# FNet and GEGLU layers on one core: issue order at the seams between token halves

## The chip, the cores and the metric

The kernel runs on one core of a Trainium2 chip. The core has TensorE (PE, matmuls into eight PSUM banks), VectorE (DVE), ScalarE (ACT), GpSimd (POOL) and SyncE (SP); the last two issue most of the transfers, which share 16 DMA engines. The metric is the device time of one execution in microseconds. The time before is the median of three runs, 1607.92 us (1604.04 to 1608.05).

## The reference

Four layers on x of 2048 tokens by 512, in fp32; the first and third mix with a discrete Fourier transform, the second and fourth are a gated feed-forward.

```python
def _A_ref(x, dft_seq_re, dft_seq_im, dft_hid_re, dft_hid_im):
    a = jnp.einsum("bsd,ed->bse", x, dft_hid_re)
    b = jnp.einsum("bsd,ed->bse", x, dft_hid_im)
    y = jnp.einsum("ts,bse->bte", dft_seq_re, a) - jnp.einsum("ts,bse->bte", dft_seq_im, b)
    return y

def _B_ref(x, w_gate, w_up, w_down):
    return (_gelu(x @ w_gate) * (x @ w_up)) @ w_down      # F = 1792

x = A_x
x = x + _A_ref(_layernorm(x), ...)
x = x + _B_ref(_layernorm(x), B_w_gate, B_w_up, B_w_down)
x = x + _A_ref(_layernorm(x), ...)
x = x + _B_ref(_layernorm(x), B_w_gate, B_w_up, B_w_down)
```

## The kernel before

**Precision.** Every fp32 operand is split in two parts of a shorter type: ScalarE copies the high part (line 151), VectorE subtracts it from the source (line 153). A product `mm3` (lines 208 to 210) is then three matmuls of 128x128 by 128x512: high by high, high by low, low by high. A split therefore costs one instruction on each of two engines, and a product of two 128-row pieces costs six matmuls.

**Layers.** Layers 0 and 2 (the numbers in the code) are the mixing layers, `mix`, 1728 matmuls each. Layers 1 and 3 are the feed-forward, `geglu(w, layer)`, called for two halves of 1024 tokens, w = 0 and 1. Matrix products are done by a Strassen scheme (Winograd's form) with seven products in place of eight: A11, A12, S1 to S4, A22 on the side of the weights, B11, B21, B22, T1 to T4 on the side of the activations.

**One half of a feed-forward layer.** The gate and up projections are 14 chunks, `up(n)`, of seven products of six matmuls (`product`, named after the weight block). The loop is skewed: `first(n + 1)` (A11 by B11, then its bank copied into another one by `seed`, line 202) and `second(n + 1)` (A12 by B21) of the next chunk are written in the middle of `up(n)`. Results leave PSUM by ScalarE copies (`copied`, line 195), gelu (line 1019) and VectorE (lines 188 and 1033). Beside the chunks, `beside(n)` runs w_down's products A11 and A12, one for each chunk; the rest of w_down, 36 products in a list `late` in layer 1 and in the first half of layer 3, comes after chunk 13. Each late product takes one piece of w_down, loaded by SP (line 327, `s<-wc`), and one split activation block, made by `prepared`. When the seven products of a kind are done, `ended` adds banks together and transposes them into the rows of x (lines 188, 1264, 191).

**The norm of a half.** For the next half, eight blocks of 128 rows of x are normed (`norm(i)` in `block_steps`): four transfers of 32 rows each load the block three norms ahead (line 245), ScalarE makes the statistics (line 564 is the first of them, lines 565, 566 and 569 follow, with two tiny POOL operations between), ScalarE applies them (line 590), VectorE transposes (line 672) and POOL writes every fourth block to memory (line 675). `fetch(c)` then reads the blocks back turned (line 686, SP), and `first(c)`, `second(c)`, `fourth(c)` and `divide` make the differences and splits for B11 to T4. These are the z blocks.

**Who runs when.** Work beside the products stands in two lists. Each `product` and each late product calls `step()`, which runs one entry of `queue`, and at every `pace[0]`-th call one entry of `slow`. In a first half, `slow` gets the eight norms with a pace of 9; in a second half before a mixing layer it gets four empty entries and the eight `terms_ahead` (the statistics for the mixing layer's first rows) with a pace of 7. After the chunks, `queue` gets the fetches and z blocks, four empty entries ahead of them. In layer 3 the fetches come already with chunk 13. At a third of the late products, eight loads of the next half's weights (`ahead`, line 1009, `s<-wb`) are laid between the entries. A rule at the end of the loop runs two entries per product where the list would otherwise outlast it.

**Order.** All this is the order in which the program is written. The build reorders it: each engine's instructions are put in the order in which a timing model finds them ready, with the written order as priority. An instruction that the model holds for ready early can so stand on its engine ahead of much that is written before it; on the chip an engine then waits at it. `tc.issue_after(ins)` ties what is written inside the block, on the engine of `ins`, to come behind `ins` on that engine; it waits for nothing else. `paced(run)` does this with the newest split on ScalarE and on VectorE. It is used before for the rows that return to the mixing layer.

Of the kernel before, what the change touches and what calls it, by code (L numbers as in the profile page):

```python
# [17 lines left out]
ND = D // P  # L18
# [19 lines left out]
FORE = {0: 4, 2: 4}  # L38
MADE = 5
LEAD = 3  # L40
NK = NS // 2
SEED_AT = 3
MIXED = 4
# [4 lines left out]
def fnet_geglu(ctx: ExitStack, tc: tile.TileContext, x_in, ws, wh, wgu, wdn, wdc, out):  # L48
# [32 lines left out]
    nc = tc.nc  # L81
# [65 lines left out]
    newest = {}  # L147
# [7 lines left out]
    def paced(run):  # L155

        def paced_run():
            with tc.issue_after(newest["ACT"].ins), tc.issue_after(newest["DVE"].ins):
                run()
        return paced_run  # L160
# [37 lines left out]
    def seed(ps, src):  # L198

        inside = id(src) in ps8.held  # L200
        with ExitStack() if inside else behind("ACT"):
            i = nc.scalar.activation(ps, src, AF.Copy)  # L202
        if inside:
            bank_read["ACT"] = i

    def mm3(ps, a, b, start, stop):
        (ah, al), (bh, bl) = a, b
        nc.tensor.matmul(ps, ah, bh, start=start, stop=False, skip_group_check=True)  # L208
        nc.tensor.matmul(ps, ah, bl, start=False, stop=False, skip_group_check=True)  # L209
        nc.tensor.matmul(ps, al, bh, start=False, stop=stop, skip_group_check=True)  # L210

    half = slice(0, 256), slice(256, 512)

# [20 lines left out]
    def x_load(layer, i, engine=nc.sync):  # L234
        t = sb.get()
        engine.dma_start(t, rows(layer, i))
        return t
# [137 lines left out]
    def make_a11(k):  # L375

        def run(v):
            held[k] = v
            return split_slot(v)
        return run  # L380
# [42 lines left out]
    def skewed(n):  # L423

        skew = SKEW[n - 2]
        return [(i, k - i * skew) for k in range(NK + (n - 1) * skew) for i in range(n) if 0 <= k - i * skew < NK]

# [14 lines left out]
    def bare(layer, b, what, k):  # L442

        return layer == 0 and b == 0 and what == "A11" and k < 6
# [4 lines left out]
    def down_order(layer, w):  # L449
        n = SEVEN[layer, w]  # L450
        up = [(name, k) for k in range(n) for name in ("A11", "A12")]
        if n < NP:
            late = [("S2", k) for k in range(n)] + [("S1", 0)] + [("S3", k) for k in range(n)] + [("S1", 1)]
            late += [("A22", k) for k in range(n - 1)] + [("S1", k) for k in range(2, n)]
            return up, late + [("A22", n - 1)] + [("S4", k) for k in range(n)]
        late = [("S1", k) for k in range(LEAD)]
        late += [p for k in range(n) for p in [("S2", k)] + [("S1", k + LEAD)] * (k + LEAD < n)]
        late.insert(LEAD + 2, up.pop())
        late += [("S4", k) for k in range(2)]
# [4 lines left out]
    def mix_items(layer):  # L464
        def raw(make, *tiles):
            items.append((F32, tiles, make, None))

        for b, what in plan(layer):
            tiles = [[ws[(b * 2 + m) * NS + k] for k in range(NS)] for m in range(2)]
            (a11, a12), (a21, a22) = ((r[:NK], r[NK:]) for r in tiles)  # L470
            hold = b >= FORE[layer]
            if what == "A11":
                for k in range(NK):
                    raw(as_is if bare(layer, b, what, k) else make_a11(k) if hold else plain, a11[k])
            elif what == "A12":
                for k in range(NK):
                    raw(plain, a12[k])
# [35 lines left out]
    queue, slow, steps_done, pace, down_making = [], [], [0], [PACE], []  # L513
# [19 lines left out]
    def norm_terms(layer, i, x, junk):  # L533
# [3 lines left out]
        shift = pool.tile([P, 1], F32, name="shift")  # L537
        if layer == 0 or layer == 2 and i >= NS - NK:
            st = spool.tile([P, 6], F32, name="st")
# [32 lines left out]
    def terms_ahead(layer, i, n):  # L572

        if i == 0:
            fresh["terms"] = x_load(layer, 0)
        x, junk = fresh.pop("terms"), sb.get()
        if i + 1 < n:
            fresh["terms"] = x_load(layer, i + 1)
        known[layer, i] = norm_terms(layer, i, x, junk)
        sb.put(x, junk)  # L580
# [23 lines left out]
    def first_rows(layer, k):  # L604
        for i in range(k if k == 0 else k + 2, min(k + 3, NK)):
            fresh[i] = x_load(layer, i)
        first_norm(layer, k)
        first_parts(k)
# [8 lines left out]
    def second_rows(layer, k):  # L617
        if NK + k not in fresh:
            fresh[NK + k] = x_load(layer, NK + k, nc.gpsimd)
        second_norm(layer, k)  # L620
        second_parts(k)
# [13 lines left out]
    def combine_late(k):  # L635
        u = t34.pop(k)
        zparts["T34", k] = split_slot(u)
        sb.put(u)
# [377 lines left out]
    def activated(g):  # L1016
# [2 lines left out]
        nc.scalar.activation(t, g, AF.Gelu_apprx_tanh)  # L1019
        return t  # L1020

    def geglu(w, layer):

        gs, h, acc = {}, {}, {0: [], 1: []}

        def finished(n, second, part, v):

            f = n // 2 * 2 + second
            if n % 2 == 0:
                gs[f, part] = activated(v)  # L1030
            else:
                t = h[f, part] = gs.pop((f, part))
                nc.vector.tensor_tensor(t, t, v, op=ALU.mult)  # L1033
# [32 lines left out]
        def product(n, ps, an, bn, start, stop):  # L1066
            step()
            hi, lo = wparts[n][an]
            for c in range(2):
                cut = slice(c * P, (c + 1) * P)  # L1070
                mm3(ps, (hi[:, cut], lo[:, cut]), blocks[bn, c], start and c == 0, stop and c == 1)
            if an in ends:
                i = ends[an]
                sb.put(*wparts[n][i])
                if not making and n + 2 < NF:
                    piece_load(n + 2, i)

        def first(n):
            if n < NF:
                chain[n] = ps8.get()  # L1080
                product(n, chain[n], "A11", "B11", True, True)
                c11[n] = ps8.get()
                seed(c11[n], chain[n])

        def second(n):
            if n < NF:
                ps = c11.pop(n)
                product(n, ps, "A12", "B21", False, True)
                finished(n, 0, 0, ps)
                ps8.put(ps)  # L1090
# [49 lines left out]
        def down(f, part):  # L1140
            for _ in down_steps(f, part):
                pass
            step()
# [134 lines left out]
        def add_rows(part, keep=False):  # L1278
            for i in range(NT):
                x_add(layer, (w * 2 + part) * NT + i, xrows.pop(0), acc[part][i], keep)  # L1280
# [39 lines left out]
        before_mix = w == 1 and layer < 3  # L1320
        plain_down = (layer, w) not in SEVEN
        if before_mix:
            slow.extend([lambda: None] * 4 + [(lambda k=k: terms_ahead(layer + 1, k, NK)) for k in range(NK)])
            pace[0] = 7
        if w == 0:
            pace[0] = PACE
            norms, others = block_steps(layer, 1)
            slow.extend(norms)
            ahead_of_all = others[:ND] if layer in (3,) else []
        if not plain_down and layer == 1 or layer == 3:  # L1330
            sb.reclaim("x")
        first(0)
        second(0)
        for n in range(NF):
            if w == 0 and n == NF - 1 and ahead_of_all:
                while slow:
# [10 lines left out]
        elif pairs == NP:  # L1347
            load_turned(0)
        if w == 0:
            queue.extend([None] * 4 + others[len(ahead_of_all):ND] + ([] if ahead_of_all else [None] * 4) + others[ND:])  # L1350
        elif before_mix:
            queue.extend((lambda k=k: first_rows(layer + 1, k)) for k in range(NK))
        ahead = [(lambda n=n, i=i: piece_load(n, i)) for n in range(2) for i in range(len(pieces))]
        if plain_down:
            for f in range(NF - LAG, NF):
                down(f, 0)
            add_rows(0)
            if before_mix:
                for k in range(NT):
                    queue.extend([lambda k=k: second_rows(layer + 1, k), lambda k=k: combine(k)])  # L1360
                queue.extend([lambda k=k: combine_late(k) for k in range(NT)])
            else:
                queue.extend(ahead)
            for f in range(NF):
                if f == NF - 2:
                    load_rows(1)
                down(f, 1)
                while len(queue) > 2 * (NF - 1 - f):
                    step()
            add_rows(1, before_mix)  # L1370
        else:
            if pairs == NP:
                pair_combined(NP - 1)
            late = down_order(layer, w)[1]
            for i, (name, k) in enumerate(late):
                for more in late[i:i + EARLY + 1]:
                    prepared(*more)
                for _ in down_product(name, k):
                    pass
                if not before_mix or i % 3 == 0:  # L1380
                    step()
                if before_mix and i == len(late) // 2:
                    stream["more"] = MORE
                if i == len(late) // 3:
                    load_turned(1)
                    if w == 0:
                        queue[:2 * len(ahead)] = [run for pair in zip(ahead, queue) for run in pair] + queue[len(ahead):2 * len(ahead)]
                while w == 0 and len(queue) > 2 * (len(late) - 1 - i):
                    step()
            if pairs < NP:  # L1390
                plain_rows()
# [24 lines left out]
    ps = ps8.get()  # L1416
# [91 lines left out]
```

## Time and profile before

| | us |
|---|---|
| median of three runs | 1607.92 |
| lowest, highest | 1604.04, 1608.05 |
| profiled execution, its own time | 1607.73 |
| its span, from first to last instruction | 1606.0 |
| TensorE busy | 1596.6 |
| VectorE, ScalarE, GpSimd busy | 1133.2, 884.5, 275.3 |
| longest transfers: pieces of w_down, 182 of 256 KB, issue to landing | 4.7 |
| mean granted clock of TensorE | 0.998 |

How to read it: a row of a timeline gives start, length, engine, line, operation, output and inputs, how many alike follow one another, and in brackets the idle time of the engine ahead of it and what ended it. `PE` rows are matmuls; their lengths overlap, so the distance of two starts is the pace. `SPq` rows are the issues of transfers by SyncE. `issue` as the reason of a wait is time for which the profile shows no releasing instruction. A row of stretches gives the busy time of each engine and the number of its instructions that touch the stretch, so that one matmul at each edge is counted in two stretches.

### The profile page before, as it was taken

Reading aid. Unit: us, or ns where it says so; the run is one execution under the profiler, and the core shown is the slowest. Engines: PE = TensorE matmul, PEld = TensorE weight load, DVE = VectorE, ACT = ScalarE, POOL = GpSimd, SP = SyncE. Lnnn points to the kernel's source line nnn. Section 1 sums busy time; section 2 is a strip of 40 time slices with the busy share of each in tenths; the row PEclk is TensorE's granted clock in tenths of the full one; section 3 lists DMA queues with packets and bytes.
Section 4 is the critical chain, followed back from the end, with each engine's and each line's share of the span. In section 5 each row is a group of like instructions: output and inputs, shape, how many; then the busy total and the mean of one; then the engine's idle time right before and its main releaser. Section 6 shows DMA issues by size and latency. Waiting matters only on the chain. (4 is left out here: it accounts for less than half of the span.)

```text
span 1606.0 us, 22616 instructions
## 1 busy us (share of the span) xinstructions
PE 1596.6 (99%) x7008; PEld 1316.2 (82%) x7008; DVE 1133.2 (71%) x1958; ACT 884.5 (55%) x1711; POOL 275.3 (17%) x469
## 2 busy tenths in 40 slices
PE   9999999999999999999999999999999999999998
PEld 7888888888888888888888888888887888888887
DVE  7997878887699783455879877777744447744574
ACT  8955565654767554546666636565545545433460
POOL 4112121352456101000040001101410000000001
PEclk9999999999999999999999999999999999999999
DMA  9878888996998899855896776878989576895445
GB/s 360 295 259 306 296 300 286 353 308 199 334 349 322 267 360 298 232 164 177 280 310 196 250 254 217 301 240 294 260 285 281 185 212 192 312 300 173 125 151 157
DMA packets 238872, 419.14 MB, mean 261 GB/s; under 512 B 28512, under 2 KB 66656, under 8 KB 237728
## 3 DMA queue, kind: packets, MB, share of 16 engines
q1 hardware_dynamic: 214512, 336.16, 65.0%
q0 software_dynamic: 24240, 81.55, 14.4%
q8 instruction: 55, 0.90, 0.2%
q14 instruction: 65, 0.53, 0.1%
HBM read 341.31 MB, written 76.28 MB: 260 GB/s over the span
## 5 line engine op out<-in xcount | busy, mean ns | idle before, releaser
L209 PE MATMUL p<-s,s 128*128 128x512 f32 x2320 | 900.2, 389 | 0.0
L210 PE MATMUL p<-s,s 128*128 128x512 f32 x2320 | 893.5, 389 | 0.0
L208 PE MATMUL p<-s,s 128*128 128x512 f32 x2320 | 868.0, 390 | 3.7 <-ACT s L195 2.3
L153 DVE TENSOR_TENSOR s<-s,s 128x512 fp32r<-128x512 f32 (+1 forms) x809 | 508.8, 663 | 127.4 <-ACT s L151 113.2
L151 ACT ACTIVATE s<-s 128x512 fp32r<-128x512 f32 (+1 forms) x809 | 455.4, 607 | 243.9 <-DVE s L184 66.4
L208 PEld LDWEIGHTS p<-s,s 128*128 128x128 f32 x2320 | 435.8, 188 | 96.9 <-ACT s L195 3.4
L209 PEld LDWEIGHTS p<-s,s 128*128 128x128 f32 x2320 | 435.8, 188 | 90.9 <-DVE s L153 0.4
L210 PEld LDWEIGHTS p<-s,s 128*128 128x128 f32 x2320 | 435.8, 188 | 90.5
L188 DVE TENSOR_TENSOR s<-s,p 128x512 f32<-128x512 f32 x188 | 127.2, 684 | 166.8 <-PE p L210 137.6
L184 DVE TENSOR_TENSOR s<-s,s 128x512 f32<-128x512 f32 (+1 forms) x374 | 223.3, 614 | 5.8 <-DMA s<-t 3.7
L195 ACT ACTIVATE s<-p 128x512 f32<-128x512 f32 x232 | 134.2, 594 | 129.7 <-PE p L210 125.9
L567 POOL TENSOR_SCALAR rstd<-rstd 128x1 f32<-128x1 f32 x40 | 24.9, 623 | 367.1 <-ACT s L566 352.2
L1019 ACT ACTIVATE s<-s 128x512 f32<-128x512 f32 x84 | 52.8, 629 | 57.9 <-DVE s L188 48.2
L153 DVE TENSOR_TENSOR s<-xwide,s 128x512 fp32r<-128x512 f32 x71 | 47.8, 681 | 35.6 <-ACT s L151 35.4
L1033 DVE TENSOR_TENSOR s<-s,p 128x512 f32<-128x512 f32 x56 | 38.4, 685 | 33.6 <-PE p L210 31.7
L313 POOL DMA_DIRECT2D wb<-s x84 | 46.2, 552 | 89.8 <-ACT s L151 67.5
L1019 ACT ACTIVATE s<-p 128x512 f32<-128x512 f32 x28 | 16.7, 597 | 67.1 <-PE p L210 65.2
L151 ACT ACTIVATE s<-xwide 128x512 fp32r<-128x512 f32 x71 | 43.2, 621 | 17.9 <-DVE xwide L184 9.4
L590 ACT ACTIVATE s<-s,shift,rstd 128x512 f32<-128x512 f32 x56 | 44.9, 811 | 10.2 <-DMA s<-x 4.8
L202 ACT ACTIVATE p<-p 128x512 f32<-128x512 f32 x56 | 32.8, 586 | 30.3 <-PE p L210 30.0
L191 DVE TENSOR_TENSOR s<-s,s 128x512 f32<-128x512 f32 (+1 forms) x68 | 40.7, 607 | 6.8 <-DMA s<-ws 4.5
L564 ACT ACTIVATE s<-s 128x512 f32<-128x512 f32 x33 | 20.7, 627 | 36.9 <-PE p L209 15.6
(100 smaller groups left out, 612.6 us busy)
## 6 DMA issues: line engine op xcount, KB each, us to landing
s<-ws SPq DMA_DIRECT2D x384, 256.0 KB, 4.9
s<-wb SPq DMA_DIRECT2D x294, 256.0 KB, 5.2
s<-wc SPq DMA_DIRECT2D x182, 256.0 KB, 4.7
s<-wh SPq DMA_DIRECT2D x116, 256.0 KB, 4.9
wb<-s POOLq DMA_DIRECT2D x98, 256.0 KB, 5.4
s<-x SPq DMA_DIRECT2D x59, 256.0 KB, 5.2
xwide<-ws SPq DMA_DIRECT2D x50, 256.0 KB, 4.9
wc<-s POOLq DMA_DIRECT2D x49, 256.0 KB, 5.1
```

The lines of the kernel that those rows point to most:

```text
L151: newest["ACT"] = nc.scalar.activation(hi, src, AF.Copy)
L153: newest["DVE"] = nc.vector.tensor_tensor(lo, src, f32(hi), op=ALU.subtract)
L184: nc.vector.tensor_tensor(out, a, b, op=ALU.subtract)
L188: bank_read["DVE"] = nc.vector.tensor_tensor(out, a, b, op=ALU.add)
L191: nc.vector.tensor_tensor(out, a, b, op=ALU.add)
L195: bank_read["ACT"] = nc.scalar.activation(v, src, AF.Copy)
L208: nc.tensor.matmul(ps, ah, bh, start=start, stop=False, skip_group_check=True)
L209: nc.tensor.matmul(ps, ah, bl, start=False, stop=False, skip_group_check=True)
L210: nc.tensor.matmul(ps, al, bh, start=False, stop=stop, skip_group_check=True)
L313: nc.gpsimd.dma_start(a, f32(t))
L590: nc.scalar.activation(z, x, AF.Identity, bias=shift, scale=rstd)
L1019: nc.scalar.activation(t, g, AF.Gelu_apprx_tanh)
```

## The change

Four places, all about order; no arithmetic changes.

```diff
+HOLD = 12
...
-        nc.tensor.matmul(ps, al, bh, start=False, stop=stop, skip_group_check=True)
+        newest["PE"] = nc.tensor.matmul(ps, al, bh, start=False, stop=stop, skip_group_check=True)
...
+    late_end = []
...
         if before_mix:
-            slow.extend([lambda: None] * 4 + [(lambda k=k: terms_ahead(layer + 1, k, NK)) for k in range(NK)])
+            slow.extend([lambda: None] * 4 + [paced(lambda k=k: terms_ahead(layer + 1, k, NK)) for k in range(NK)])
             pace[0] = 7
         if w == 0:
             pace[0] = PACE
             norms, others = block_steps(layer, 1)
-            slow.extend(norms)
+            slow.extend(paced(run) if layer == 3 else run for run in norms)
...
-        first(0)
-        second(0)
+        with tc.issue_after(late_end.pop().ins) if late_end else ExitStack():
+            first(0)
+            second(0)
...
         if w == 0:
-            queue.extend([None] * 4 + others[len(ahead_of_all):ND] + ([] if ahead_of_all else [None] * 4) + others[ND:])
+            queue.extend([None] * 9 + others[len(ahead_of_all):ND] + ([] if ahead_of_all else [None] * 4) + others[ND:])
...
                 for _ in down_product(name, k):
                     pass
+                if i == len(late) - HOLD:
+                    late_end.append(newest["PE"])
```

- The norms of layer 3's first half (which prepare its second) and the statistics ahead of the mixing layer, in layer 1's second half, are `paced`: on ScalarE and VectorE they come behind the newest split that is written before them.
- The z blocks (in layer 1 with their fetches) are written five steps later in the late products.
- `first(0)` and `second(0)` of a half come, on TensorE, behind the last matmul of the late product that is twelfth from the end in the list of the half before (number 24 of 0 to 35). A matmul is noted in every half; what layer 1's second half notes is used by layer 3's first half, a whole mixing layer later, and that of the last half by none.

## The prediction

> **What bounds the kernel now.** I read the page's head first, then the busy time of each engine in stretches that I cut where TensorE stops being full, and then the order of time around each cut.
>
> ```profile
> span 1606.0 us, 22616 instructions
> PE 1596.6 (99%) x7008; PEld 1316.2 (82%) x7008; DVE 1133.2 (71%) x1958; ACT 884.5 (55%) x1711; POOL 275.3 (17%) x469
> ```
>
> ```profile
> 0.00:40.00 40.00, 38.65 (x149) 28.22 (x150) 31.90 (x79) 33.41 (x63) 19.31 (x42) 1.00 0.99 359
> 40.00:400.00 360.00, 360.00 (x1590) 298.10 (x1589) 303.50 (x531) 216.18 (x421) 87.94 (x135) 1.00 0.84 290
> 400.00:440.00 40.00, 39.91 (x177) 32.72 (x176) 27.74 (x52) 30.70 (x65) 18.79 (x36) 1.00 1.01 325
> 440.00:760.00 320.00, 320.00 (x1414) 264.96 (x1413) 214.70 (x367) 182.80 (x367) 70.58 (x118) 1.00 0.83 271
> 760.00:800.00 40.00, 39.23 (x173) 32.20 (x172) 35.35 (x61) 26.61 (x49) 0.00 (x0) 1.00 0.84 294
> 800.00:1200.00 400.00, 400.00 (x1766) 331.07 (x1765) 302.20 (x535) 222.83 (x437) 60.01 (x106) 1.00 0.79 259
> 1200.00:1240.00 40.00, 37.69 (x160) 30.64 (x158) 14.96 (x23) 20.27 (x44) 3.72 (x7) 0.96 1.07 283
> 1240.00:1360.00 120.00, 120.00 (x531) 99.38 (x530) 66.01 (x102) 58.63 (x109) 2.84 (x7) 1.00 0.64 196
> 1360.00:1400.00 40.00, 39.47 (x175) 32.27 (x174) 33.98 (x56) 21.94 (x40) 0.00 (x0) 1.00 0.90 315
> 1400.00:1600.00 200.00, 200.00 (x884) 165.62 (x883) 100.16 (x154) 71.10 (x125) 12.12 (x20) 1.00 0.61 184
> 1600.00:1606.00 6.00, 1.64 (x8) 1.02 (x6) 2.66 (x4) 0.00 (x0) 0.00 (x0) 0.80 0.64 249
> ```
>
> The columns are length, then busy time and count of PE, weight loads, DVE, ACT and POOL, then granted clock, DMA share and GB/s. The number of matmuls is fixed, and in full stretches they start 400/1764 = 0.2268 us apart (1766 less the two at the edges). So the time is 7008 matmuls plus whatever TensorE waits, and between the opening and the tail it waits in four stretches only: those at 400, 760, 1200 and 1360. The one at 1200 is by far the largest (160 matmuls where 178 fit), and the only one with a clock below full. Nothing that keeps TensorE fed elsewhere can gain anything; any new wait costs its whole length.
>
> The stretch at 1200, on ScalarE and then on TensorE:
>
> ```profile
> 1217.17 0.57 ACT L1019 ACTIVATE s<-p 128x512 f32<-128x512 f32 x1
> 1222.25 0.63 ACT L564 ACTIVATE s<-s 128x512 f32<-128x512 f32 x1 [4.51 <-issue]
> 1222.88 0.58 ACT L195 ACTIVATE s<-p 128x512 f32<-128x512 f32 x1
> ```
>
> ```profile
> 1220.82 0.39 PE L210 MATMUL p<-s,s 128*128 128x512 f32 x1
> 1223.51 0.50 PE L208 MATMUL p<-s,s 128*128 128x512 f32 x1 [2.31 <-ACT s L195]
> ...
> 1224.81 0.63 PE L210 MATMUL p<-s,s 128*128 128x512 f32 x1
> ...
> 1227.80 0.79 PE L208 MATMUL p<-s,s 128*128 128x512 f32 x2
> 1228.43 0.40 PE L209 MATMUL p<-s,s 128*128 128x512 f32 x1
> ```
>
> ```profile
> 1216.51 7.15 SPq L245 DMA_DIRECT2D s<-x  x8
> ```
>
> ScalarE stands idle for 4.51 us ahead of line 564, the first statistic of a norm, while the copy of a finished PSUM bank (line 195) stands behind it. TensorE needs that bank. The norm reads rows of x by line 245, whose eight issues take until 1223.66. So a norm that is wanted much later came to the head of ScalarE's queue before its rows had landed.
>
> **The change, part by part.** It adds and removes no instruction of any engine; it adds order alone.
>
> *Norms of layer 3's second half.* Where are they wanted? The last matmul starts 0.39 before 1601.64, at 1601.25. Layer 3 has 882 + 894 = 1776 matmuls (14 chunks of 42, then 49 w_down products of 6; in the second half 35 of 6 and 96 of plain rows). At 0.2268 that is 402.8, and with some 5 us of waits (below) layer 3 starts at 1601.3 - 402.8 - 5.0 = 1193.5. A norm runs at every 9th step; a chunk has 7 steps and 48 matmuls (42 in the first).
>
> ```profile
> L564 ACT ACTIVATE s<-s x8: 617/632/634, 1184.6 to 1281.0; 128x512 f32<-128x512 f32 x8
> ```
>
> The eight are spread from 1184.6 to 1281.0; the one at 1222.25 is the fifth, by the timeline's order. The fifth norm's step is the 37th to 45th, that is after 42 + 4x48 = 234 to about 300 matmuls: 1247 to 1266. It ran 25 to 44 us early. With the change it stands on ScalarE behind the newest split, that of A11 of pair 2, whose data are finished in chunk 4 (42 + 3x48 + 30 = 216 matmuls, 1242 at the earliest). Its rows were all issued by 1223.66, so it would no longer find them missing, and the bank copies of chunks 2 to 4 no longer stand behind it.
>
> What goes with that wait, from the rows: 1223.51 - 1220.82 - 0.227 = 2.46; then five starts in 1.30 where 1.13 is usual, 0.17; then nine starts from 1224.81 to 1228.43, 3.62 where 2.04 is usual, 1.58. Together **4.21 us**. The last piece is the clock:
>
> ```profile
> 1224.80:1228.20 3.40, 3.40 (x10) 2.60 (x9) 1.96 (x4) 2.08 (x5) 0.52 (x1) 0.51 1.02 222
> ```
>
> By the Trainium skill (TensorE: Matmul & The Clock Gate, "Part 1: The HAM clock gate"), the clock halves after an idle window of about 3.4 us, free-running, and matmuls of 512 columns then start 426.7 ns apart; the trace agrees on the pitch (1224.81 to 1225.24 and on, 0.43), but here a wait of under 2.7 us was enough. By the page's window the stall would be worth 2.46 + 0.17 = 2.6 and the sum below would end at 1604.3; I go by the rows.
>
> Cost of the move itself: eight norms of about five ScalarE operations, four DMAs each for their rows (not held back, since they are SP's) and a transpose on DVE go to 1202 to 1310, where ACT is busy 58.6 of 120 and DVE 66.0. Behind a held norm on ScalarE stand only bank copies and gelus, and the norm waits for a split that comes before them in the program anyway. Bounds: 0, or again one wait of 4.21 if some other late input now stands at the head. I take 0. The last norm then ends some 23 us later than 1281, near 1305, and its block is fetched from chunk 13, at about 1193.5 + 4 + 618x0.2268 = 1338: 33 us of room.
>
> *Statistics ahead of the mixing layer* (layer 1, second half, 600 to 730): TensorE is full from 440 to 760, so this can gain nothing there; ACT is busy 182.8 of 320, so it costs nothing either. Taken at 0; bounds 0 and one wait of 1.04 (the price of the wait at 766, below).
>
> *Blocks of the next half five steps later.* A step comes with each late product, 6 x 0.2268 = 1.36, so 6.8 us. In layer 1 the last split before the second half (1601.3 - 402.8 - 5.0, less 1728 + 882 matmuls and a wait of 1.04: 600.5) is
>
> ```profile
> 594.88 0.69 DVE L153 TENSOR_TENSOR s<-s,s 128x512 fp32r<-128x512 f32 x1
> ```
>
> Even if that is the last block it ends at 595.6 + 6.8 = 602.4, and in the order of the program S1 needs its block 18 matmuls into the half, at 604.6. The cover is the row of A22 products at the end of the late stage (7 x 1.36 = 9.5 us). 0, and if the cover were gone, 6.8 per half at most.
>
> *First products behind the twelfth late product from the end.* This is where the order on TensorE changes. The late stage of layer 3 before:
>
> ```profile
> 1348.00:1360.00 12.00, 12.00 (x55) 9.93 (x54) 11.55 (x20) 6.29 (x12) 0.00 (x0) 1.00 0.90 286
> 1360.00:1372.00 12.00, 11.47 (x51) 9.10 (x50) 12.00 (x21) 8.81 (x18) 0.00 (x0) 1.00 1.05 386
> 1372.00:1380.00 8.00, 8.00 (x37) 6.62 (x36) 7.61 (x14) 6.33 (x13) 0.00 (x0) 1.00 0.91 317
> 1380.00:1392.00 12.00, 12.00 (x54) 9.95 (x53) 7.28 (x12) 5.40 (x9) 0.00 (x0) 1.00 0.68 216
> ```
>
> ```profile
> L202 ACT ACTIVATE p<-p x2: 579/588/597, 1364.0 to 1396.6; 128x512 f32<-128x512 f32 x2
> ```
>
> ```profile
> L202 ACT ACTIVATE p<-p x2: 582/582/582, 586.8 to 598.1; 128x512 f32<-128x512 f32 x2
> ```
>
> Line 202 copies a first product into the bank of the next: its rows date the next half's first product at 1364.0 and, in layer 1, at 586.8. The halves begin by count at 1193.5 + 882x0.2268 + 5 = 1398.5 and 600.5, and twelve products before are 1382.2 and 584.2. So the hold bites in layer 3, by 18 us or more, and hardly in layer 1. There DVE is full from 1348 to 1380 and DMA above 0.9; the wait in this stretch is for a piece of w_down:
>
> ```profile
> 1362.65 0.61 PE L208 MATMUL p<-s,s 128*128 128x512 f32 x2
> 1363.79 0.50 PE L208 MATMUL p<-s,s 128*128 128x512 f32 x1 [0.53 <-DMA s<-wc]
> ```
>
> ```profile
> 1356.29 3.30 SPq L327 DMA_DIRECT2D s<-wc  x5
> 1359.71 1.03 SPq L1009 DMA_DIRECT2D s<-wb  x2
> ```
>
> Lost: 1363.79 - 1362.88 - 0.23 = 0.68, and 0.11 at the next start, 0.8. Its loads (line 327) are issued between those of the next half, each when its buffer is released by DVE or ACT. With block work five steps down in priority, DVE's eleven or so block operations of 1348 to 1360 make room for the late splits, the buffers come free sooner, and TensorE needs no filler. Bounds: a gain of 0.8; a loss of the filler, between the 6 matmuls that must lie ahead of 1364.0 (1.4 us) and the 30 that the program puts ahead of the second seed at 1396.6 (6.8 us). I take the gain, since DVE has 4.7 of 12 us free from 1380 to 1392, where the moved work goes.
>
> The third wait stays as it is:
>
> ```profile
> 764.29 1.07 PE L208 MATMUL p<-s,s 128*128 128x512 f32 x4
> 766.12 0.50 PE L208 MATMUL p<-s,s 128*128 128x512 f32 x1 [0.77 <-DMA s<-wc]
> ```
>
> (766.12 - 764.97 - 0.23 + 0.11 = 1.04; no hold applies there.)
>
> **The sum.** Own time of the profiled execution 1607.73 (span 1606.0 and 1.73 around it) - 4.21 - 0.80 = 1602.7. The median of the runs, 1607.92, is 0.2 above the profiled one, so I say **1602.8**, 0.32% below the median. A measurement of this kernel tells about 0.3% from no change, 4.8 us, so the forecast stands just beyond that line.
>
> **The rivals.** *Only the norm's wait goes*: the wait for w_down stays or moves, and small new ones come, as any new order brings: 1603.5 and up to 1607, no change that can be told. For it: DMA is at 1.05 from 1360, whatever the order on TensorE. Against it: the load in question was late in issue, not only in transfer.
>
> *The cover is lost* (the other side): with the next half's products held, TensorE runs into late products whose splits or pieces are not there. Place: 1361 to 1375, and the like in layer 1; price 6.8 + 1.4, and after each the slow clock, 1.75 as above: 1607.7 - 4.2 + 8.2 + 3.5 = 1615.2. It decides as soon as the late splits on DVE fall more than the two or three products that are ready in advance (about 4 us) behind. For it: DVE at 12.00 of 12. Against it: the block work that fills DVE is pushed back by 6.8 us at the same time. By the page above, waits this short would leave the clock alone, and this case would be 1611.7.
>
> *The pin does not hold*: the newest split could itself run early, the fifth norm with it, and the wait stays: 1607. Against it: that split needs chunk 4's product.
>
> **How the numbers follow.** Forecast 0.48 (1601.7, with the wait at 766 gone too, to 1603.1), only the norm's wait 0.22, pin without effect 0.06, cover lost 0.24. Faster by over 0.3% 0.47, within 0.28, slower 0.25. The range: the lowest is 1601.7, and a run more or less favourable (the runs shown reach from 1604.0 to 1608.1) takes it to 1600.5; above it takes in the second and third case and the smaller losses of the cover, to 1613. The likeliest case alone: 1601 to 1604.
>
> **What would show it.** Right: the stretch 1200 to 1240 with 178 matmuls at clock 1.00, line 564's fifth row after 1240, no 4.51 ahead of it; line 202's first row of the second half after 1380, and no wait for wc near 1363. Wrong: line 195 or 564 again ahead of a matmul; a wait for line 153 or for wc between 1360 and 1400; a clock below 1.00 in any slice after the opening.

## The result, and the profile after

| | before | after |
|---|---|---|
| median, us (nine runs each, the first three of before included) | 1607.92 | 1602.85 |
| lowest to highest | 1604.04 to 1609.71 | 1601.86 to 1604.44 |
| profiled span | 1606.0 | 1601.0 |

The ratio of the times is 0.9971, with a 95% interval of 0.9961 to 0.9981. The forecast was 1602.8. The busy time by stretch of the changed kernel, cut at the same places (length, then PE, weight loads, DVE, ACT, POOL, granted clock, DMA share, GB/s):

```profile
span 1601.0 us, 22648 instructions
```

```profile
400.00:440.00 40.00, 39.91 (x176) 32.73 (x176) 27.74 (x52) 30.70 (x65) 18.73 (x36) 1.00 1.01 320
440.00:760.00 320.00, 320.00 (x1414) 265.05 (x1413) 214.64 (x368) 183.04 (x366) 69.60 (x117) 1.00 0.84 271
760.00:800.00 40.00, 39.29 (x174) 32.20 (x173) 34.69 (x60) 26.47 (x49) 0.00 (x0) 1.00 0.86 295
800.00:1200.00 400.00, 400.00 (x1766) 331.09 (x1765) 301.52 (x535) 221.22 (x430) 57.99 (x104) 1.00 0.78 259
1200.00:1240.00 40.00, 40.00 (x178) 33.12 (x177) 18.96 (x28) 21.22 (x46) 2.85 (x7) 1.00 0.95 246
1240.00:1360.00 120.00, 120.00 (x531) 99.41 (x530) 68.10 (x106) 63.79 (x123) 3.57 (x9) 1.00 0.72 228
1360.00:1400.00 40.00, 40.00 (x178) 33.15 (x177) 31.38 (x51) 15.87 (x28) 2.64 (x4) 1.00 0.90 307
```

Two of the four stretches in which TensorE waited are full now: that at 1200 (178 matmuls for 160, clock 1.00) and that at 1360. Those at 400 and 760 are as they were. Below are the fifth statistic of layer 3's norms, on ScalarE (line 565 now, since the code lies one to six lines lower), and the copies of the first products of the next halves, in layer 3 and in layer 1 (line 203 was 202):

```profile
1240.93 0.63 ACT L152 ACTIVATE s<-s 128x512 fp32r<-128x512 f32 x1 [1.48 <-DVE s L1036]
1241.46 0.61 ACT L565 ACTIVATE s<-s 128x512 f32<-128x512 f32 x1
```

```profile
L203 ACT ACTIVATE p<-p x2: 582/582/582, 1387.0 to 1387.8; 128x512 f32<-128x512 f32 x2
L203 ACT ACTIVATE p<-p x2: 582/582/582, 593.1 to 594.7; 128x512 f32<-128x512 f32 x2
```

The statistic stands right behind a split and waits for nothing, 19 us later than before. The first copy of layer 3's second half moved from 1364.0 to 1387.0, that of layer 1's from 586.8 to 593.1. In layer 1 it was the later blocks that moved it, not the hold: without the hold it is at 593.4 (run 3), without the later blocks at 586.7 (run 4). Which part bought the time is another matter.

### The profile page after: what moved, and what is told of

Its sections match the earlier page's. It is cut to its first block, busy times and chain, and to the rows that moved or that the text cites. A ratio compares the mean times of both kernels' runs of the same rounds, so it can differ in the third digit from the quotient of the medians.

```text
span 1601.0 us, 22648 instructions
## 1 busy us (share of the span) xinstructions
PE 1594.2 (100%) x7008; PEld 1315.2 (82%) x7008; DVE 1132.7 (71%) x1958; ACT 883.7 (55%) x1711; POOL 271.5 (17%) x469
## 4 chain that ended last, share of the span: by engine, by line
PE 93%; DMA 3%; issue 2%; POOL 1%; ACT 0%; DVE 0%; SPq 0%; POOLq 0%; ACTq 0%; DVEq 0%
PE p L210 31%; PE p L211 31%; PE p L209 31%; DMA s<-t 1%; PE p L810 1%; DMA s<-x 1%; DMA s<-ws 0%; DMA s<-wc 0%; POOL rstd L568 0%; DMA xwide<-ws 0%; ACT s L152 0%; POOL s L687 0%; POOL wb L314 0%; DVE s L154 0%; ACT xwide L196 0%
## 5 line engine op out<-in xcount | busy, mean ns | idle before, releaser
L1020 ACT ACTIVATE s<-s 128x512 f32<-128x512 f32 x84 | 52.8, 629 | 47.1 <-DVE s L189 44.6
L980 POOL DMA_DIRECT2D wc<-s x42 | 30.5, 728 | 53.8 <-ACT s L152 36.4
```

## The experiments

Ratios are to runs of the kernel before on the same chip; where no interval is given there is one run and its profile. "By starts" means the distance of two starts less the usual 0.23 us. In the fourteen profiles the 201st matmul starts between 51.6 and 52.3 us, though no edit touches what comes before it: a difference under 0.7 us between the spans of two single executions tells nothing. "The stretch at 1200" is the wait behind line 564, "at 1360" the wait for a piece of w_down.

**1. The pin on layer 3's norms alone.**

```diff
-            slow.extend(norms)
+            slow.extend(paced(run) if layer == 3 else run for run in norms)
```

> The kernel before with the pin on layer 3's norms alone. My theory (the pin takes 4.2 us, the later blocks with the held products 0.8): about 1603.5 us, TensorE full from 1200 to 1240 at clock 1.00, and a wait of 0.5 to 1 us for a piece of w_down (wc) still there near 1360. Rival A (the pin alone does everything, by its shift of the schedule): 1602.8 and no wait near 1360. Rival B (the norm's wait goes because of the later blocks or the held products): no better than 1607.

1603.11 us, ratio 0.9977 (0.9967 to 0.9987).

```profile
1200.00:1240.00 40.00, 40.00 (x178) 33.15 (x177) 18.20 (x27) 19.24 (x39) 1.50 (x4) 1.00 1.03 267
1360.00:1400.00 40.00, 40.00 (x178) 33.15 (x177) 28.71 (x47) 17.25 (x30) 2.64 (x4) 1.00 0.88 305
```

Both stretches are full. Rival A holds: with the pin alone neither wait is there, so the later blocks and the hold are not needed for the one at 1360 to go. (Run 8 shows that this wait can also be missing without the pin.)

**2. All but that pin.**

```diff
-            slow.extend(paced(run) if layer == 3 else run for run in norms)
+            slow.extend(norms)
```

> The kernel after without the pin on layer 3's norms. My theory: the wait of about 2.5 us for the bank copy behind line 564 is back near 1223 with the slow clock behind it, the wait near 1360 stays gone: about 1607 us. Rival B (other parts of the change removed it): no such wait, 1603 us.

1602.78 us, ratio 0.9970 (0.9960 to 0.9979): my theory missed this one. The wait is gone without the pin. The list of ScalarE shows how:

```profile
1221.93 0.58 ACT L203 ACTIVATE p<-p 128x512 f32<-128x512 f32 x1 [0.16 <-PE p L211]
...
1227.19 0.63 ACT L152 ACTIVATE s<-s 128x512 fp32r<-128x512 f32 x1 [1.19 <-DVE s L1036]
1227.88 0.63 ACT L565 ACTIVATE s<-s 128x512 f32<-128x512 f32 x1
```

The fifth statistic is still early, but it starts at 1227.88 and not at 1222.25, and it finds its rows there (no wait in brackets). The rest of the change moved it by 5.6 us without meaning to. Its rows came sooner too: the last of its four transfers was issued at 1214.07 and landed at 1218.22; before it was issued at 1214.30 and landed at 1222.18.

**3. All but the hold.**

```diff
-        with tc.issue_after(late_end.pop().ins) if late_end else ExitStack():
+        with ExitStack():
```

> The kernel after without the hold on the next half's first products. My theory: the later blocks already let the late splits through, so no wait of TensorE near 1360 even with the first product early (line 202's first row near 1360): the span within 0.3 us of the changed kernel's 1601.0. Rival C (the hold is what removes the wait, since the early first product and its weights crowd out w_down's pieces): a wait for wc of 0.5 to 1 us comes back between 1350 and 1370, span about 1601.8.

1603.26 us in one run, span 1601.5, 0.5 over the change's where I had allowed 0.3. The first product is early again (line 203's first row at 1362.9), and TensorE has no wait at 1360. So nothing here speaks for rival C, that the early first product delays the piece of w_down. The wait at 766 is 0.5 us longer (1.2 us for wc, 0.7 with the change), a place that no part of the change names; it also differs by 0.3 us between profiles whose order up to there is the same (0.77 before, 0.45 in run 1).

**4. All but the later blocks.**

```diff
-            queue.extend([None] * 9 + others[len(ahead_of_all):ND] + ([] if ahead_of_all else [None] * 4) + others[ND:])
+            queue.extend([None] * 4 + others[len(ahead_of_all):ND] + ([] if ahead_of_all else [None] * 4) + others[ND:])
```

> The kernel after with the blocks at their old place (four empty steps). My theory: DVE is again full of block work ahead of the late splits, and with the first products held TensorE has less to fill with: a wait between 1350 and 1380 of 0.8 to 5 us, span 1601.8 to 1606. Rival C (the hold alone does it): no wait, span 1601.0.

1603.97 us in one run, span 1602.2:

```profile
1356.95 0.61 PE L209 MATMUL p<-s,s 128*128 128x512 f32 x2
1358.22 0.50 PE L209 MATMUL p<-s,s 128*128 128x512 f32 x1 [0.66 <-DMA s<-wc]
```

A wait for wc is back at this seam, 0.8 us by starts (1358.22 - 1357.18 - 0.23). Run 9, which has both pins but no hold, has none. This fits a hold that makes the wait and later blocks that pay for it, but it rests on one profile each.

**5. The pin on the fifth norm only.**

```diff
-            slow.extend(norms)
+            slow.extend(paced(run) if layer == 3 and k == 4 else run for k, run in enumerate(norms))
```

> The kernel before with the pin on the fifth of layer 3's eight norms alone. Theory D (the wait is a meeting of one early statistic with one late block of rows; whatever puts that one statistic later removes it): no wait near 1223, clock 1.00 from 1200 to 1240, about 1603.5 us, a wait for wc near 1360 left or not. Rival (the pin works by the shift of all eight norms, or another norm takes the fifth's place at the head): a wait of 2 us or more between 1200 and 1280 is left, 1606 us or more.

1603.70 us, ratio 0.9968 (0.9957 to 0.9980). No wait at 1200 and none at 1360; one statistic of eight is enough, so the price was that of a single meeting. Here the last of its rows landed at 1224.97, no sooner than before, but the statistic stood at 1252.17: it is its place that counts. But the profiled execution (1605.15) has a wait that before's did not show, in layer 1:

```profile
635.41 0.63 ACT L564 ACTIVATE s<-s 128x512 f32<-128x512 f32 x1 [6.11 <-DMA s<-x]
```

```profile
PE p L208 <- ACT s L151: 1.7, 1, 1.7
```

This is the first of the statistics ahead of the mixing layer, at the head of ScalarE 6 us ahead of its row; ScalarE worked almost without a pause after it, and the split that TensorE needed came late. Up to 1170 every engine has the order of the kernel before, by line, operation and tile, so up to here these are two executions of one order: the row was issued at 629.08 here and at 625.58 before, and landed about 6 us later in both.

**6 and 7. The later blocks alone, the hold alone.** Each is its line of the diff in the kernel before.

> The kernel before with the later blocks alone. Theory D: moving the blocks in layer 1 shifts the order of all that follows, so that the fifth statistic, though not pinned, starts after its rows have landed, as it did without the pin (statistic at 1227.9, rows at 1218.2): no wait near 1223, about 1603 us. Rival (the hold on the first products or the pinned statistics did that): the wait near 1223 is there, 1607 us.

1605.68 us, ratio 0.9990 (0.9979 to 1.0000).

```profile
1200.00:1240.00 40.00, 40.00 (x178) 33.08 (x177) 15.18 (x22) 24.53 (x52) 5.18 (x11) 1.00 1.01 303
600.00:640.00 40.00, 36.48 (x154) 29.71 (x153) 13.99 (x21) 13.85 (x30) 6.17 (x12) 0.96 1.06 291
```

As theory D said, the stretch at 1200 is full without any pin; the time is not the 1603 that it gave. The gain is lost again at 634.90, where a bank copy stood behind the first statistic of layer 1 (6.46 us on its row) and TensorE waited 3.5 us, with the slow clock after it.

> The kernel before with the hold on the first products alone. Theory D: the order of layer 3's norms is that of the kernel before, so the wait near 1223 stays, with the slow clock: 1605 to 1608 us. With the blocks at their old place and the first products held, the wait for wc near 1360 stays too (0.8) or grows. Rival (the hold shifts the schedule enough): no wait near 1223, 1603 us.

1608.97 us in one run. The waits of TensorE in it (who waited for whom, in all, times, longest):

```profile
PE p L209 <- ACT s L196: 2.1, 1, 2.1
PE p L209 <- DMA s<-wc: 2.0, 2, 1.2
```

The wait at 1200 stays, that at 1360 is 1.4 by starts where it was 0.8, and one of 0.8 by starts stands at 633. The time lies a little above what I expected, but within the runs of the kernel before on that chip (1604.94 to 1612.05): that the hold alone loses is not shown.

**8. The pin on layer 1's statistics alone.**

```diff
-            slow.extend([lambda: None] * 4 + [(lambda k=k: terms_ahead(layer + 1, k, NK)) for k in range(NK)])
+            slow.extend([lambda: None] * 4 + [paced(lambda k=k: terms_ahead(layer + 1, k, NK)) for k in range(NK)])
```

> The kernel before with the pinned statistics ahead of the mixing layer alone. I hold that they neither gain nor cost: TensorE full from 600 to 760 as before, the wait near 766 between 0.7 and 1.5 us, and the wait near 1223 still there with the slow clock: 1605 to 1608 us. Rival: they are what moves the wait near 1223, 1603 us.

1605.41 us in one run. The wait near 1223 is there, shorter (1.5 us), and the slow clock that I expected with it did not come but for a matmul or two:

```profile
1221.54 0.39 PE L210 MATMUL p<-s,s 128*128 128x512 f32 x1
1223.42 0.50 PE L208 MATMUL p<-s,s 128*128 128x512 f32 x1 [1.49 <-ACT s L195]
```

From 740 to the end this kernel has the order of the kernel before on every engine, by line, operation and tile. So the same order cost a wait of 1.65 us by starts here, and 2.46 with the slow clock behind it, 4.21 in all, in the profile before. And the wait at 1360 is not there: the only wait of TensorE for a piece of w_down in the whole execution is that at 766 (in all, times, longest).

```profile
PE p L208 <- DMA s<-wc: 0.7, 1, 0.7
```

**9. Both pins, without hold and later blocks.**

> The kernel before with both pins (layer 3's norms, and the statistics ahead of the mixing layer), without the hold and with the blocks at their old place. Theory E (the pins do all of it: a statistic at the head of ScalarE ahead of its rows is the only thing that costs more than 1 us, once near 1223 and, in some executions, near 633): 1602.5 to 1603.3 us, all runs within 3 us of each other, no wait near 1360 as with the norms' pin alone. Rival F (the hold and the later blocks carry part of the gain): 1604 us or more.

1603.33 us, ratio 0.9975 (0.9964 to 0.9986), the runs within 2 us (1602.74 to 1604.66), no wait at 633, 1223 or 1360. The interval overlaps that of the whole change, so no contribution of the hold and the later blocks together can be told.

**10. All but the pin on layer 1's statistics.**

> The kernel after without the pin on the statistics ahead of the mixing layer. Theory E: the first of them waits on ScalarE for its row again (issued near 625, landed 5.7 to 8.2 us later in the runs so far), and in some executions TensorE waits 1 to 5 us near 633: median 1603 to 1605, runs 3 us or more apart. My prediction's view (this pin is worth nothing): 1602.8, spread as with the change.

1604.63 us, ratio 0.9980 (0.9972 to 0.9989); runs from 1603.53 to 1605.97, so the median is as theory E said and the spread, 2.4, less. On ScalarE and TensorE:

```profile
631.35 0.63 ACT L565 ACTIVATE s<-s 128x512 f32<-128x512 f32 x1 [4.04 <-DMA s<-x]
631.89 0.19 ACT L565 ACTIVATION_READ_ACCUMULATOR s<-s 128x1 f32 x1
631.98 0.58 ACT L196 ACTIVATE s<-p 128x512 f32<-128x512 f32 x1
```

```profile
631.13 0.39 PE L211 MATMUL p<-s,s 128*128 128x512 f32 x1
632.61 0.50 PE L209 MATMUL p<-s,s 128*128 128x512 f32 x1 [1.09 <-ACT s L196]
```

It is the picture of 1223 once more, statistic, bank copy, matmul: 1.25 us by starts. This pin takes away a wait that my prediction put at nothing. What it is worth in the median is not settled: the interval overlaps those of the whole change and of run 9, and in this profile 0.8 us more than with the change went to the wait at 766, which the pin does not touch.

**11. The norms of layer 1's first half pinned too** (an attempt at the wait near 405).

```diff
-            slow.extend(paced(run) if layer == 3 else run for run in norms)
+            slow.extend(paced(run) for run in norms)
```

> The kernel after with the norms of layer 1's first half pinned as well. If the wait near 405 (0.36 us after a bank copy that stands behind a norm's statistic written later) has the same cause, it goes, and the time is 0.4 to 0.5 us less: 1602.4 us. Rival (the wait there comes from the copies of the mixing layer's rows, or the moved norms make another): as the change, 1602.8, or up to 2 us more.

1604.72 us, ratio 0.9979 (0.9970 to 0.9988): 1.9 us above the change by medians, with intervals that overlap. The stretch 400 to 440 is full, so the cause was guessed rightly, but two new waits came:

```profile
585.89 0.50 PE L209 MATMUL p<-s,s 128*128 128x512 f32 x1 [0.95 <-DMA s<-wc]
...
588.60 0.50 PE L209 MATMUL p<-s,s 128*128 128x512 f32 x1 [1.05 <-DMA s<-wc]
```

They are for pieces of w_down in layer 1's late stage, 2.3 us by starts. What was saved is less than half a microsecond: before, two starts near 405 stand 0.48 and 0.34 us apart where 0.23 is usual, 0.36 in all.

**12. The hold behind the very last late product** (`HOLD = 1`).

> The kernel after with the next half's first products held behind the very last late product (HOLD = 1). Rival case of the prediction (the cover is lost) should show here if anywhere: a wait of 1.5 us or more between 1350 and 1400 or 580 and 605, span 1602.5 to 1608. My theory: other products (S1 of the first chunk, which needs no first product, and A22) fill in, no such wait, span 1600.8 to 1601.8.

1602.79 us in one run, span 1601.0.

```profile
560.00:600.00 40.00, 40.00 (x178) 33.14 (x177) 37.49 (x62) 19.92 (x35) 0.85 (x2) 1.00 0.92 323
1360.00:1400.00 40.00, 40.00 (x178) 33.12 (x177) 31.59 (x52) 15.30 (x27) 3.62 (x6) 1.00 0.90 301
```

TensorE is full at both seams; the cover that the prediction feared to lose isn't needed. The run moves the second copy of layer 3's second half by 10 us (1398.2 for 1387.8), the first by 0.8 only.

No kernel tried beats the change beyond the intervals.

## Why the prediction was right, and where it was not

**The pin on layer 3's norms: right in its mechanism.** The stretch it names is full, the clock stays at 1.00, and runs 1 and 5 show that the pin, even on one statistic, suffices. It isn't the only way: runs 2 and 6 lose the wait by a chance shift of the same statistic. The mechanism is thus a meeting of one early instruction with one late transfer; the queue's order at that one place decides, and many edits can disturb it. The size, 4.21 us, is that of one execution: run 8, with the same order, waited 1.65 and had the slow clock for a matmul or two at most.

The prediction took the wrong transfers for the late ones. The eight issues from 1216.51 are the rows of later norms; they landed from 1223.08 on, when the statistic had already run. The fifth norm's last piece was issued before them:

```profile
1214.30 0.31 SPq L245 DMA_DIRECT2D s<-x  x1
```

It took 7.88 us and landed at 1222.18, and the statistic started at 1222.25. Runs 7 and 8 have the same 0.07 us between the two (1222.84 and 1222.91, 1222.09 and 1222.16), so the wait that the profile calls `issue` was for this piece. The eight norms also moved less than was forecast: they start at 1187.4 to 1285.0 with the change, not from 1202 on and to about 1305; nothing in the sum hangs on it.

**The 0.8 us at 1360: right in the sum, wrong in its cause.** The step that failed was that "with block work five steps down in priority" the buffers come free sooner. Runs 1, 5, 8 and 9 have no such wait with the blocks at their old place and no hold. What the runs show in its place: this wait comes and goes between executions of one order, since run 8 has the order of the kernel before from 740 on and does not have it. The two profiles of a hold without later blocks have it (runs 4 and 7: 0.8 and 1.4), those of a hold with them have not. That would fit two edits that cancel; why the kernel before had the wait in its one profile stays open.

**The statistics of layer 1: a step that failed.** I took them at 0, since TensorE was full from 440 to 760 in the profile. But ScalarE's own row in the kernel before already showed the first one waiting:

```profile
631.43 0.63 ACT L564 ACTIVATE s<-s 128x512 f32<-128x512 f32 x1 [2.36 <-DMA s<-x]
```

In that execution 2.36 us of idle ScalarE cost nothing, nor did 2.82 in run 1; in others it was 4.0 to 6.5 us, and TensorE then waited 0.8 to 3.7 us by starts (in runs 5, 6, 7 and 10). So four of the six profiles without the pin show the wait, and none of the eight with it. Between run 10 and the whole change lie 1.8 us of median, though with run 1, which lacks this pin and reached 1603.11, the worth is not always that. Two places where the arrival of a row decides may also be part of the spread of the kernel before, up to 1612.05 in the other sessions against 1606.11 for any kernel with both pins; no run shows that by itself.

**The sum** came out within 0.1 us, and partly by luck: it added one wait from a profile that shows a single execution, a second one whose removal I gave to the wrong edits, and left a third out. Its last step also rounds downwards: 1607.73 - 4.21 - 0.80 and the 0.19 to the median make 1602.9. And the range ends at 1613, below the 1615.2 that it gives for its own rival.

**The rivals.** Cover lost: not seen with the change, whose seams are full, nor in run 12. The pin without effect: refuted by the statistic's row at 1241.46 and by run 1. "Only the norm's wait goes" came closest among them in its view that small waits move whenever the order does: run 11 (586, 588) is an example. The wait at 766 shows that they move without a new order too.

## What to carry to other kernels

When the engine that bounds the time is 99% busy, look at the other engines' rows with idle time on a transfer at the head of their queue, and ask what stands behind them: an operation needed 20 us later that is placed early because a model thinks its data are there can stop the work behind it whenever the transfer is late. Tying it behind an instruction that is near its use took the wait away wherever it was done here; run 11, which tied more, got new waits. And a stretch that is full in one profile isn't safe: where the margin is the few microseconds by which transfers vary, time several executions.

## What the runs showed of the hardware

Rows landed later where the DMA engines were busier. These are the rows of line 245, 64 KB each, from issue to landing (minimum, median, maximum), first in 1178 to 1190, then in 1204 to 1232 of the kernel before, where the DMA share was 0.59 and 1.07:

```profile
DMA to landing us min/median/max: 1.7/1.9/5.5
```

```profile
DMA to landing us min/median/max: 4.1/5.5/7.9
```

The clock: after waits with 1.88 us from one start to the next (run 8) and 2.09 (run 5) the matmuls went on at the usual pace, but for one or two; after 2.46 (run 7), 2.69 (before) and 3.90 (run 6) some eight starts came at 0.43 us. For these five waits the edge lies between 2.1 and 2.5 us; whether it is the same at every moment, five waits do not show. The Trainium skill (TensorE: Matmul & The Clock Gate, "Part 1: The HAM clock gate") gives an idle window of about 3.4 us, free-running, and starts 426.7 ns apart at half the clock. The pace of the slow matmuls agrees, 0.43 us; the waits of 2.46 and 2.69 us are shorter than that window and brought it all the same, and here the measurement counts.
